# Reordering the first transfers, warming the array, widening the first stage and simplifying the first eight steps of a fused FNet and MLP kernel

## The chip, the cores and the metric

The kernel runs on one core of one Trainium2 chip. The metric is the device time of one execution in microseconds (us), as the median of several executions. Every run of a changed kernel is set against runs of the kernel before on the same chip in the same rounds. The engines are called PE (TensorE; PEld is its weight load), DVE (VectorE), ACT (ScalarE), POOL (GpSimd) and SP (the queue that issues most transfers).

## The reference

```python
# x (8, 3008, 256) float32; w_in (256, 2048) and w_out (2048, 256) are float64
X = np.fft.fft(np.fft.fft(x, axis=1), axis=2)
x = X.real.astype(np.float32).reshape(8 * 3008, 256)
h = x @ w_in
g = h * (1.0 / (1.0 + np.exp(-1.702 * h)))
out = (g @ w_out).astype(np.float32)
```

The random weights are scaled in float64 (NumPy promotes them) and arrive as float64. The kernel reads them as pairs of 32-bit words and rounds them to float32 on the chip.

## The kernel before

The sequence transform (3008 = 94 x 32) is split into a first stage, with 94 rows on the partitions and folded by symmetry, and a second stage of 32 points. The second transform, over the 256 columns, is folded into `w_in`: `fold_w` multiplies each rounded 512-column chunk of it by cosines and sines. Then 384 steps (8 batches x 3 blocks x 2 halves x 8 parts) compute 256 hidden units each and add their share to the output.

Weights come in eight chunks of 1 MB, four "in" and four "out". Each is rounded by five DVE operations with one ACT and two POOL operations around them:

```python
def bounds(key):
    hi = raw[key][:, :, 1].bitcast(F32)
    ...
    nc.scalar.activation(g[:], hi, ACTF.Square)
    nc.gpsimd.tensor_scalar(m[:], hi, scalar1=TOP, scalar2=-TOP, op0=ALU.min, op1=ALU.max)

def rounded(out, key):
    ...
    dve.scalar_tensor_tensor(m[:], g[:], LOW * LOW, m[:], op0=ALU.is_ge, op1=ALU.mult)
    dve.tensor_scalar(a[:], bits, scalar1=3, ...)                 # exponent
    dve.scalar_tensor_tensor(a[:], bits, 0xC0000000, a[:], ...)   # sign
    dve.scalar_tensor_tensor(a[:], lo, 29, a[:], ...)             # low bits
    dve.tensor_scalar(bits, lo, scalar1=28, scalar2=1, ...)       # round-up bit
    return lambda: nc.gpsimd.tensor_tensor(out.bitcast(U32), a[:], bits, op=ALU.add)
```

The first stage of batch 0 folds into `el` and `eu` (buffers of the pool `hp`, four in all) and multiplies with 96 columns of 94 rows:

```python
nc.tensor.matmul(ps[0:96, ...], lhsT=w1[:, l0, :], rhs=el[:, q, c0:c1], start=True, stop=False)
nc.tensor.matmul(ps[0:96, ...], lhsT=upper, rhs=eu[:, 3 - q, c0:c1], start=False, stop=True)
```

A step consists of `hidden(t)`, `product(t-2)`, `activate(t)` and, at the end of a half, `combine`. The order of these calls is the order of the instructions on each engine.

```python
def hidden(t):                       # pa, pb: 4 + 4 matmuls of 128x256
    ...
    nc.scalar.copy(v[:], pa[:])
    nc.vector.tensor_tensor(h[:, 0]..., v[:], pb[:], op=ALU.add)
    sums(t - 1)                      # Strassen's sums: two on POOL, two on DVE
    ...                              # two dif, one more h, all DVE
def product(t):                      # 7 products, 14 matmuls of 128x128, on wo and its differences wt
def combine(t):                      # 7 DVE operations at the end of each half of 8 steps

for t in range(n + LAG):
    hidden(t); product(t - LAG); activate(t); combine(t - LAG)   # guards cut
    for fn, args in extra.get(t, ()):                            # rounding, later batches
        fn(*args)
```

The start-up, before step 0:

```python
# w1, w1x on the ACT queue; then
load_first()                         # all of x[0], SP queue
load_in(0, nc.scalar); nc.scalar.dma_start(out=small[:], in_=tab2)
load_in(1, nc.scalar); load_out(0, nc.scalar)
...                                  # four times fold_first, mix_first
shuffle_first()                      # 12 transfers, SP
bounds(("in", 0)); bounds(("in", 1)); round_in(0); finish_in(0)
load_in(2, nc.sync)
fold_w(0)
...                                  # rounding of in 1 and out 0, second stage
```

Of the kernel before, what the change touches and what calls it, by code (L numbers as in the profile page):

```python
# [87 lines left out]
def kernel(ctx: ExitStack, tc, x, w_in, w_out, tab1, tab2, out):  # L88
# [22 lines left out]

    w1 = const.tile([NA, NW, 96], F32, tag="w1", name="w1")
    small = const.tile([128, 2 * 128 + 128 + 4 * H], F32, tag="small", name="small")
# [7 lines left out]
    af2 = const.tile([128, NF], F32, tag="af2", name="af2")  # L121
    ones = const.tile([1, 128], F32, tag="ones", name="ones")

    def bank(name):
# [49 lines left out]
    def mix1(b, c):  # L174
        full = xt[b]
        t, e = full[0:NA], e0.get(b)
        ps = bank("ps1")
        for i in range(2):
            jj, o = 2 * c + i, i * D
            if jj:  # L180
                nc.tensor.matmul(ps[0:96, o:o + D], lhsT=w1[:, jj, :], rhs=t[:, NB - jj, :], start=True, stop=True)  # L181
                continue
            for l0, l1, c0, c1 in ((0, 16, 0, H + 1), (17, 18, H + 1, D)):
                nc.tensor.matmul(ps[0:96, c0:c1], lhsT=w1[:, l0, :], rhs=e[:, 0, c0:c1], start=True, stop=False)
                nc.tensor.matmul(ps[0:96, c0:c1], lhsT=w1[:, l1, :], rhs=e[:, 1, c0:c1], start=False, stop=True)

        nc.scalar.copy(full[:, 2 * c:2 * c + 2, :].rearrange("p j d -> p (j d)"), ps[0:96, :])  # L187
# [3 lines left out]

    def load_first():
        t = xt[0] = xp.tile([96, NB, D], F32, tag="x", name="xt")
        src = x[0].rearrange("(p j) d -> p j d", j=NB)
        for c in range(4):
            for lo, hi in (((0, 4), (29, 32), (16, 17)), ((4, 8), (25, 29)), ((8, 12), (21, 25)), ((12, 16), (17, 21)))[c]:
                for p0, p1 in PIECES:
                    nc.sync.dma_start(out=t[p0:p1, lo:hi, :], in_=src[p0:p1, lo:hi, :])

    def fold_first(c):  # L200

        t = xt[0]
        el, eu = (hp.tile([NA, 4, D], F32, tag="h", name=n) for n in ("el", "eu"))
        e4[c] = el, eu
        first = 29 - 4 * c
        runs = [(el, 0, 4 * c, 4, False)]
        runs += [(eu, 0, first, 4, True)] if c else [(eu, 0, first, 3, True), (eu, 3, 16, 1, False)]
        for e, i, lo, n, flip in runs:
            fwd, rev = free(t[0:NA], lo * D + 1, [D, n], [1, H - 1]), free(t[0:NA], lo * D + D - 1, [D, n], [-1, H - 1])
            nc.gpsimd.tensor_copy(free(e[:], i * D, [D, n], [H, 2]), free(t[0:NA], lo * D, [D, n], [H, 2]))  # L210
            nc.vector.tensor_tensor(e[:, i:i + n, 1:H], fwd, rev, op=ALU.add)
            nc.vector.tensor_tensor(e[:, i:i + n, H + 1:D], *((rev, fwd) if flip else (fwd, rev)), op=ALU.subtract)

    def mix_first(c):
        ps = bank("ps1")
        el, eu = e4[c // 2]
        for i in range(2):
            jj, o = 2 * c + i, i * D
            q = jj % 4
            ends = ((0, 16, 0, H + 1), (17, 18, H + 1, D)) if jj == 0 else ((jj, NW + jj - 1, 0, D),)  # L220
            for l0, l1, c0, c1 in ends:
                upper = w1[:, l1, :] if l1 < NW else w1x[:, l1 - NW, :]
                nc.tensor.matmul(ps[0:96, o + c0:o + c1], lhsT=w1[:, l0, :], rhs=el[:, q, c0:c1], start=True, stop=False)
                nc.tensor.matmul(ps[0:96, o + c0:o + c1], lhsT=upper, rhs=eu[:, 3 - q, c0:c1], start=False, stop=True)
        nc.scalar.copy(xt[0][:, 2 * c:2 * c + 2, :].rearrange("p j d -> p (j d)"), ps[0:96, :])

    def shuffle_first():
        t4 = t4t[0] = tp.tile([128, NG, D], F32, tag="t4", name="t4")
        for a in range(NG):
            nc.sync.dma_start(out=t4[:, a, :], in_=xt[0][8 * a:8 * a + 8, 0:16, :])  # L230

# [51 lines left out]
    def bounds(key):  # L283


        hi = raw[key][:, :, 1].bitcast(F32)
        g = sp.tile([128, 1024], F32, tag="s", bufs=3, name="g")
        m = cv.tile([128, 1024], F32, tag="m", bufs=2, name="m")
        nc.scalar.activation(g[:], hi, ACTF.Square)
        nc.gpsimd.tensor_scalar(m[:], hi, scalar1=TOP, scalar2=-TOP, op0=ALU.min, op1=ALU.max)  # L290
        pre[key] = g, m

    def rounded(out, key):

        t, (g, m) = raw.pop(key), pre.pop(key)
        lo, bits = t[:, :, 0], m[:].bitcast(U32)
        a = cv.tile([128, 1024], U32, tag="a", name="a")
        dve = nc.vector
        dve.scalar_tensor_tensor(m[:], g[:], LOW * LOW, m[:], op0=ALU.is_ge, op1=ALU.mult)

        dve.tensor_scalar(a[:], bits, scalar1=3, scalar2=0x3FFFFFF8, op0=ALU.logical_shift_left, op1=ALU.bitwise_and)
        dve.scalar_tensor_tensor(a[:], bits, 0xC0000000, a[:], op0=ALU.bitwise_and, op1=ALU.bitwise_or)
        dve.scalar_tensor_tensor(a[:], lo, 29, a[:], op0=ALU.logical_shift_right, op1=ALU.bitwise_or)
        dve.tensor_scalar(bits, lo, scalar1=28, scalar2=1, op0=ALU.logical_shift_right, op1=ALU.bitwise_and)
        return lambda: nc.gpsimd.tensor_tensor(out.bitcast(U32), a[:], bits, op=ALU.add)

# [13 lines left out]

    def finish_out(n):
        ps = slice(2 * n, 2 * n + 2)
        last["out", n]()
        b11, b12, b21, b22 = (wo[:, ps, q, :] for q in range(4))
# [52 lines left out]
    def sums(t):  # L377

        if not 0 <= t < len(steps):
            return  # L380
# [9 lines left out]
    def product(t):  # L390
        b, blk, hh, p = steps[t]
        if p == 0:
            for n in range(4):
                pot[n] = pso.tile([128, 2, 2, H], F32, tag=f"o{n}", name=f"po{n}")
        h, s = ht.pop(t), st.pop(t)

# [13 lines left out]
    def combine(t):  # L410
# [5 lines left out]
        if hh == 0:  # L416
            for sg in range(2):
                ot[sg] = op.tile([128, 4, D], F32, tag="os", name="os")
        u2, u3, u4 = (op.tile([128, 2, H], F32, tag=f"u{n}", bufs=1, name=f"u{n}") for n in (1, 2, 3))
        c1 = pot["c"]  # L420
# [22 lines left out]
    assert NCK == 4  # L443
    w1x = tp.tile([128, NG, D], F32, tag="t4", name="w1x")[0:NA].rearrange("p a d -> p (a d)")[:, 0:NX * 96]
    w1x = w1x.rearrange("p (j n) -> p j n", j=NX)
    for p0, p1 in PIECES:
        nc.scalar.dma_start(out=w1[p0:p1], in_=tab1[p0:p1, 0:NW])
    for p0, p1 in PIECES:
        nc.scalar.dma_start(out=w1x[p0:p1], in_=tab1[p0:p1, NW:])
    load_first()  # L450
    load_in(0, nc.scalar)
    nc.scalar.dma_start(out=small[:], in_=tab2)
    load_in(1, nc.scalar)
    load_out(0, nc.scalar)
    nc.vector.memset(ones[:], 1.0)
    for c in range(4):
# [5 lines left out]
    mix_first(7)  # L462
    shuffle_first()
    bounds(("in", 0))
    bounds(("in", 1))
    round_in(0)
    finish_in(0)
    load_in(2, nc.sync)
    fold_w(0)
    bounds(("out", 0))  # L470
    round_in(1)
    finish_in(1)
    load_out(1, nc.sync)
    nyquist_weights(0)
    bounds(("in", 2))
    round_out(0)
    finish_out(0)
    load_in(3, nc.sync)
    rotate(0, 0, 4, nc.scalar.copy)
    for cs in range(2):  # L480
        stage2(0, 0, cs)
    nyquist(0, 0)

    extra = {}
# [5 lines left out]

    at(0, round_in, 2)
    at(0, load_out, 2, nc.sync)
    at(0, bounds, ("out", 1))
    at(1, fold_w, 1)
    at(1, nyquist_weights, 1)
    at(1, rotate, 0, 4, NG)
    at(1, finish_in, 2)
    at(1, round_out, 1)
    at(1, load_out, 3, nc.sync)
    at(1, bounds, ("in", 3))  # L500
    if B > 1:
        at(1, turn, 1, 17, 32)
        at(1, load_x, 1)
    at(2, finish_out, 1)
    at(2, round_in, 3)
    at(2, bounds, ("out", 2))
    at(3, fold_w, 2)
    at(3, nyquist_weights, 2)
    at(3, finish_in, 3)
    at(3, round_out, 2)  # L510
    at(3, bounds, ("out", 3))
    at(4, finish_out, 2)
    at(4, round_out, 3)
    at(5, fold_w, 3)
    at(5, nyquist_weights, 3)
    at(5, finish_out, 3)
    for b in range(B):
        t0 = b * NBLK * NF
        if b + 2 < B:
            at(t0 + 10, turn, b + 2, 17, 32)  # L520
        if b + 1 < B:
            for c in range(NCH):
                at(t0 + 7 + 2 * c, fold1, b + 1, c, nc.gpsimd)
                at(t0 + 8 + 2 * c, mix1, b + 1, c)
            at(t0 + 24, spill, b + 1)
            at(t0 + 29, fill, b + 1)
            if b + 2 < B:
                at(t0 + 33, load_x, b + 2)
            at(t0 + 38, rotate, b + 1)
        for blk in range(NBLK):  # L530
# [47 lines left out]
```

## Time and profile before

| | before |
|-|-|
| median of three runs | 2133.01 us (2132.48 to 2133.05) |
| span of the profiled run | 2130.3 us |
| end of stage 1 (end of its last matmul) | 41.1 us |
| first matmul of `fold_w` | 51.27 us |
| first matmul of step 6 | 146.32 us |

First the head of the page: busy us, share of the span and number of instructions for each engine. Below it are two of the rows that cut the span into 40 slices of 53 us, with the busy share (or, for PEclk, the granted clock) in tenths.

```profile
PE 2039.4 (96%) x14626; PEld 1912.7 (90%) x14626; DVE 1438.3 (68%) x2707; ACT 673.6 (32%) x952; POOL 774.7 (36%) x1058
...
PE   5669999999999999999999999999999999999998
...
PEclk9789999999999999999999999999999999999999
```

The average says that PE is the limit. The slices say that this holds from the fourth on; in the first three PE is busy five to six tenths. A change to the start-up is worth what it moves the beginning of the fourth slice.

The list of waits gives who waited for whom, then total us, times and the longest.

```profile
PE po L403 <- DVE u L426: 21.7, 16, 2.0
```

PE waits sixteen times, up to 2.0 us each, for the operations of `combine` on DVE; there are 48 halves, so every third of them has such a stall.

### The profile page before, as it was taken

How to read it: one execution, taken by the hardware profiler on the slowest of the kernel's cores; microseconds unless marked ns; L12 is line 12 of the kernel's file. 1: busy time of each engine (PE TensorE's matmuls, PEld its weight loads, DVE VectorE, ACT ScalarE, POOL GpSimd, SP SyncE). 2: the span in 40 equal slices, each digit the busy share in tenths (PEclk: the TensorE clock that was granted, in tenths of full speed). 3: DMA queues.
4: the chain of work that ended last, by engine and by line, in shares of the span. 5: the costliest groups of instructions: out<-in, count | busy, mean ns of one | idle time of the engine just before them, and what ended most of it. 6: DMA issues, size and time to landing. Idle time of an engine off the chain costs nothing.

```text
span 2130.3 us, 36302 instructions
## 1 busy us (share of the span) xinstructions
PE 2039.4 (96%) x14626; PEld 1912.7 (90%) x14626; DVE 1438.3 (68%) x2707; ACT 673.6 (32%) x952; POOL 774.7 (36%) x1058
## 2 busy tenths in 40 slices
PE   5669999999999999999999999999999999999998
PEld 3459999989999999999999899999999989999997
DVE  3676766766766667666666766676666667676666
ACT  1223323333233333333333333333333333323332
POOL 2465422353224522254223532244322542222222
PEclk9789999999999999999999999999999999999999
DMA  6341151123322033211431124111332112101200
GB/s 164 118 108 6 50 109 11 47 25 64 79 30 28 20 65 80 51 6 50 79 40 47 10 49 110 6 49 24 65 79 25 6 43 49 18 21 8 22 21 20
DMA packets 43263, 101.43 MB, mean 48 GB/s; under 512 B 4969, under 2 KB 27879, under 8 KB 41107
## 3 DMA queue, kind: packets, MB, share of 16 engines
q1 hardware_dynamic: 41631, 94.27, 24.0%
q10 hardware_dynamic: 1464, 4.83, 0.8%
q8 instruction: 115, 1.88, 0.4%
q14 instruction: 53, 0.43, 0.1%
HBM read 55.83 MB, written 45.76 MB: 48 GB/s over the span
## 4 chain that ended last, share of the span: by engine, by line
DVE 43%; PE 33%; issue 12%; ACT 9%; DMA 2%; SPq 1%; ACTq 0%; DVEq 0%; POOL 0%
PE po L403 19%; DVE dif L368 10%; DVE h L363 8%; DVE h L370 8%; DVE s L387 7%; DVE s L388 7%; ACT v L362 6%; PE pa L356 5%; PE pb L356 5%; DVE u L426 1%; PE ps L181 1%; DVE os L426 1%; ACT xt L187 1%; PE ps L253 1%; ACT pq L255 1%
## 5 line engine op out<-in xcount | busy, mean ns | idle before, releaser
L375 ACT ACTIVATE h<-h 128x1024 f32<-128x1024 f32 x384 | 405.9, 1057 | 1369.6 <-DVE h L370 1345.4
L385 POOL TENSOR_TENSOR s<-h 128x256 f32<-128x256 f32 x384 | 281.2, 732 | 1273.1 <-issue 930.7
L363 DVE TENSOR_TENSOR h<-v,pb 128x512 f32<-128x512 f32 x384 | 263.9, 687 | 614.8 <-ACT v L362 574.0
L403 PE MATMUL po<-wt,s 128*128 128x128 f32 x4608 | 644.5, 276 | 1.1 <-DVE s L387 1.1
L403 PEld LDWEIGHTS po<-wt,s 128*128 128x128 f32 x4608 | 580.5, 193 | 1.3 <-DVE s L387 1.3
L403 PE MATMUL po<-wo,h 128*128 128x128 f32 x3072 | 473.5, 277 | 23.2 <-DVE u L426 21.7
L403 PEld LDWEIGHTS po<-wo,h 128*128 128x128 f32 x3072 | 432.3, 192 | 56.6 <-DVE u L426 38.5
L356 PE MATMUL pa<-pq,wcs 128*128 128x256 f32 x1536 | 400.9, 384 | 0.0
L356 PE MATMUL pb<-pq,wcs 128*128 128x256 f32 x1536 | 397.9, 382 | 0.0
L368 DVE SCALAR_TENSOR_TENSOR dif<-nb,af,pb 128x256 f32<-128x256 f32 x768 | 332.0, 473 | 0.0
L356 PEld LDWEIGHTS pb<-pq,wcs 128*128 128x128 f32 x1536 | 294.8, 192 | 40.6
L356 PEld LDWEIGHTS pa<-pq,wcs 128*128 128x128 f32 x1536 | 268.5, 193 | 25.4 <-issue 1.5
L370 DVE TENSOR_TENSOR h<-v,dif 128x512 f32<-128x512 f32 x384 | 276.6, 720 | 13.2
L386 POOL TENSOR_TENSOR s<-h 128x256 f32<-128x256 f32 x384 | 283.4, 738 | 0.0
L387 DVE TENSOR_TENSOR s<-s,h 128x256 f32<-128x256 f32 x384 | 250.8, 653 | 2.0 <-POOL s L385 2.0
L403 PE MATMUL po<-wo,s 128*128 128x128 f32 x1536 | 234.8, 276 | 0.0
L403 PE MATMUL po<-wt,h 128*128 128x128 f32 x1536 | 234.6, 275 | 0.0
L362 ACT COPY v<-pa 128x512 f32<-128x512 f32 x384 | 219.4, 571 | 6.0 <-PE pa L356 6.0
L388 DVE TENSOR_TENSOR s<-h,s 128x256 f32<-128x256 f32 x384 | 206.6, 538 | 13.2
L403 PEld LDWEIGHTS po<-wo,s 128*128 128x128 f32 x1536 | 202.8, 193 | 0.0
L403 PEld LDWEIGHTS po<-wt,h 128*128 128x128 f32 x1536 | 202.7, 192 | 0.0
L169 POOL TENSOR_TENSOR xt<-xt 94x510 f32<-94x510 f32 (+1 forms) x56 | 73.8, 1318 | 4.4
(64 smaller groups left out, 749.4 us busy)
## 6 DMA issues: line engine op xcount, KB each, us to landing
out_dram<-os SPq DMA_DIRECT2D x176, 128.0 KB
Td<-xt SPq DMA_DIRECT2D x7, 1536.0 KB
t<-Td SPq DMA_DIRECT2D x7, 1536.0 KB
Xr<-in_x_dram SPq DMA_DIRECT2D x7, 1410.0 KB
xt<-in_x_dram SPq DMA_DIRECT2D x7, 1280.0 KB
xt<-Xr SPq DMA_DIRECT2D x7, 1200.0 KB
nb<-pq SPq DMA_DIRECT2D x23, 256.0 KB
raw<-in_moe_w_out_dram SPq DMA_DIRECT2D x3, 1024.0 KB
```

The costliest lines, as they stand in the source:

```text
L169: eng.tensor_tensor(low, low, free(t, up + D - 1, [-D, n], [-1, D - 1]), op=ALU.add)
L356: nc.tensor.matmul(ps[:, i * 256:(i + 1) * 256], lhsT=wcs[cs][:, f * 128:(f + 1) * 128], rhs=pq[:, cs, ks], start=True, stop=True)
L362: nc.scalar.copy(v[:], pa[:])
L363: nc.vector.tensor_tensor(h[:, 0].rearrange("p f k -> p (f k)"), v[:], pb[:], op=ALU.add)
L368: nc.vector.scalar_tensor_tensor(dif[:, c], nb[:, ks], af2[:, f:f + 1], pb[:, c], op0=ALU.mult, op1=ALU.subtract)
L370: nc.vector.tensor_tensor(free(h[:], 512 + NB - 1, [NB, 16], [-1, NB]), v[:].rearrange("p (a k) -> p a k", k=NB), dif[:].rearrange("p (a k ...
L375: nc.scalar.activation(ht[t][:], ht[t][:], ACTF.Gelu_apprx_sigmoid)
L385: nc.gpsimd.tensor_tensor(s1, a21, a22, op=ALU.add)
L386: nc.gpsimd.tensor_tensor(s3, a11, a21, op=ALU.subtract)
L387: nc.vector.tensor_tensor(s2, s1, a11, op=ALU.subtract)
L388: nc.vector.tensor_tensor(s4, a12, s2, op=ALU.subtract)
L403: nc.tensor.matmul(pot[n][:, i, q, :], lhsT=lhs[:, q * 128:(q + 1) * 128], rhs=rhs, start=(p == 0 and i == 0 and q == 0), stop=(p == NP - ...
```

## The change

The intent is to shorten the start-up:

- the first weight chunk is loaded ahead of `x` and rounded before stage 1; `small`, the second "in" chunk and the first "out" chunk are issued behind `x`, all on SP;
- eight matmuls on a tile of ones warm the array, and the first stage's weights are 128 columns wide;
- the two low-bit operations of the rounding leave DVE and become two ACT copies; the small fold copies go from POOL to ACT;
- the first eight steps use plain products (eight matmuls of 128x256) without Strassen's sums, and the differences `wt` move to steps 7 to 10;
- the folding of batch 1 in the background is shifted by three steps (its rotation by one step later; the rotation of the later batches moves two steps earlier).

```diff
+    load_in(0, nc.sync)
     for p0, p1 in PIECES:
-        nc.scalar.dma_start(out=w1[p0:p1], in_=tab1[p0:p1, 0:NW])
+        nc.scalar.dma_start(out=w1[p0:p1, 0:NW * 96], ...)
+    load_first(0)
     ...
+    for c in range(1, 4):
+        load_first(c)
+    nc.sync.dma_start(out=small[:], in_=tab2)
+    load_in(1, nc.sync)
+    load_out(0, nc.sync)
+    warm(8)
+    bounds(("in", 0))
+    round_in(0)
+    finish_in(0)
@@ mix_first
-                nc.tensor.matmul(ps[0:96, ...], lhsT=w1[:, l0, :], ...)
+                nc.tensor.matmul(ps[:, ...], lhsT=mat(w1, l0, 128), ...)
@@ bounds, rounded
+        nc.scalar.activation(r[:].bitcast(F32), lo, ACTF.Copy, scale=2.0 ** -29, bias=2.0 ** 23)
+        nc.scalar.activation(r[:], r[:].bitcast(F32), ACTF.Copy, bias=-2.0 ** 23)
-        dve.scalar_tensor_tensor(a[:], lo, 29, a[:], ...)
-        dve.tensor_scalar(bits, lo, scalar1=28, scalar2=1, ...)
@@ product
+        if t < NP:
+            ... 8 matmuls of 128x256: h[:, half, f] x wo[:, p, 2f:2f+2]
+            return
@@ combine
+        if t < NP:
+            ... two nc.scalar.copy
+            return
@@ background work of batch 1
+        late = 0 if b else 3
-                at(t0 + 7 + 2 * c, fold1, b + 1, c, nc.gpsimd)
+                at(t0 + 7 + 2 * c + late, fold1, b + 1, c, nc.gpsimd)
```

(Cut: the rest of the schedule of rounding, the zeroing of 32 columns behind the tables, two shuffles issued from ACT.)

## The prediction

> **What bounds the kernel now.** I read the page's head and 40 slices first: PE is busy 96% of 2130.3 us, and only the first three slices (some 160 us) are thin. Then I cut the span into windows; columns are window, length, then busy us with instruction counts for PE, PEld, DVE, ACT and POOL, then the granted clock, DMA share and GB/s.
>
> ```profile
> 20.00:40.00 20.00, 19.42 (x46) 12.55 (x45) 7.35 (x8) 5.25 (x8) 5.05 (x6) 1.00 0.60 170
> 40.00:60.00 20.00, 8.87 (x29) 4.52 (x27) 12.07 (x12) 4.99 (x7) 7.11 (x3) 1.00 0.35 74
> 60.00:80.00 20.00, 11.10 (x28) 7.80 (x29) 6.64 (x9) 5.60 (x8) 7.32 (x7) 0.57 0.51 163
> 80.00:100.00 20.00, 10.22 (x36) 7.50 (x35) 14.99 (x16) 5.48 (x9) 8.25 (x6) 0.66 0.18 52
> 100.00:120.00 20.00, 10.41 (x64) 7.94 (x62) 19.69 (x20) 3.23 (x4) 14.20 (x10) 0.82 0.90 245
> 120.00:140.00 20.00, 16.79 (x88) 13.67 (x88) 17.82 (x19) 4.72 (x8) 13.79 (x11) 0.84 0.39 108
> ...
> 160.00:180.00 20.00, 20.00 (x154) 19.12 (x153) 13.27 (x27) 7.88 (x13) 9.82 (x15) 1.00 0.02 2
> ...
> 500.00:1000.00 500.00, 493.54 (x3618) 468.24 (x3618) 341.43 (x657) 164.10 (x232) 185.66 (x262) 1.00 0.26 46
> ```
>
> From 160 us on, PE is busy 98% (1939 of 1970 us, summing all later windows), so that part ends when PE has done its work; nothing in the diff takes PE work out of it. The first 160 us are a start-up in which PE mostly waits. The whole question is how much earlier the saturated part begins. As marker I take the instant at which PE starts the two 128x256 groups `pa` of step 6 (last one that needs a freshly folded weight chunk): 146.32 us in the timeline below. From there PE runs without a gap at 4.85 us a step.
>
> The timeline of the start (start us, duration, engine, line, what, count, idle before and releaser):
>
> ```profile
> 26.34 1.06 PE L223 MATMUL ps<-el,w 94*96 94x256 f32 x2
> 27.19 1.06 PE L224 MATMUL ps<-eu,w1x 94*96 94x256 f32 x2
> ...
> 51.27 5.44 PE L333 MATMUL psw<-wst,small 128*128 128x512 f32 x8 [10.20 <-POOL wst L305]
> ...
> 58.80 1.12 SPq L273 DMA_DIRECT2D raw<-in_moe_w_in_dram  x1
> ...
> 67.00 1.12 ACT L289 ACTIVATE g<-raw 128x1024 f32<-128x1024 f32 x1 [8.36 <-DMA raw<-in_moe_w_in_dram]
> ...
> 68.02 0.15 ACT L245 COPY t<-psr 128x4 f32<-128x4 f32 x1
> ...
> 75.08 0.58 ACT L362 COPY v<-pa 128x512 f32<-128x512 f32 x1 [1.42 <-PE pa L356]
> ...
> 81.55 1.63 DVE L302 SCALAR_TENSOR_TENSOR a<-m,a 128x1024 uint32<-128x1024 uint32 x1
> 83.21 1.23 DVE L303 SCALAR_TENSOR_TENSOR a<-raw,a 128x1024 uint32<-128x1024 uint32 x1
> 84.36 0.69 DVE L304 TENSOR_SCALAR m<-raw 128x1024 uint32<-128x1024 uint32 x1
> ...
> 85.19 2.34 POOL L305 TENSOR_TENSOR wst<-a,m 128x1024 uint32<-128x1024 uint32 x1 [3.09 <-DVE m L304]
> 85.55 2.26 DVE L387 TENSOR_TENSOR s<-s,h 128x256 f32<-128x256 f32 x1
> ...
> 146.32 2.08 PE L356 MATMUL pa<-pq,wcs 128*128 128x256 f32 x4
> ```
>
> The reader is to see four things. (1) The first stage's 94x256 matmuls start 0.85 us apart, while the same form in the saturated part (L181) takes 0.43; stage 1 therefore lasts to 41.1 us. (2) Step 0 begins late: ScalarE sits behind a 1 MB weight chunk issued at 58.80 (it lands at 67.0), and the tiny copy at 68.02, which the second stage needs, stands behind it in order. (3) Step 0's `v` copy comes at 75.08. (4) Steps 0 to 6 take 71.2 us (75.08 to 146.32) because VectorE rounds weight chunks between the steps: five operations, 1.2+0.7..1.2+1.2..1.6+1.2..1.6+0.7 = about 5.9 us a chunk, plus its `s` operation of 0.42 stretched to 2.26 under GpSimd's 2.34 us addition. The wait list says the same: PE's largest wait is for the folded weights.
>
> ```profile
> PE psa L339 <- ACT wcs L334: 27.8, 4, 11.0
> ```
>
> **What the Trainium skill says.** "TensorE: Matmul & The Clock Gate", Part 1 (the HAM clock gate): the array runs at half rate until it has been busy for about 3.4 us and falls back after an idle window. The trace agrees at L333: its eight halves are 0.85 apart for about 3.5 us, then 0.43. It does not agree for stage 1, 27 us of unbroken 94x96 work at half rate (and the clock column calls that window 1.00). I read this as 96 of 128 columns being too little activity to release the gate; no page says so. The same page, Architectural detail: ScalarE is a strict FIFO; the 68.02 copy shows it. "SBUF — State Buffer", on the shared port pair: a GpSimd operation holds the pair for its whole length and a VectorE one with two SBUF inputs blocks; 85.55 shows it (2.26 for 0.42). "DMA: Bandwidth & Descriptors", Issuing engines are not separate DMA queues: SP and ACT feed the same 16 engines, so reordering helps only by what goes first; the first 20 us agree, with the DMA share at 0.93.
>
> **The change part by part.**
>
> *First transfers.* The first weight chunk goes ahead of x, and the second weight chunk, `small` and the first output chunk go behind it. Bytes up to the last piece of x: 1.05 + 0.67 + 0.53 + 3.08 = 5.3 MB; at the 226 to 300 GB/s of the first 30 us that is 20 to 23 us plus start and landing, so about 25.5 us against 31.15 before. Chunk 0 of x is later, though (7.8 before; 11 to 13.5 now, behind 1 MB), and VectorE first does three roundings (9.3 to 13.8), so stage 1 starts at about 15 to 17 rather than 8.6 to 13.
>
> *Warming and width.* Eight warm-up matmuls of 128x512: four halves cold, twelve warm, about 1.5 to 10 us, off the path. A gap of about 5 us follows, so I expect chunk 0 of stage 1 to begin cold and turn warm within 4 us if 128 columns are enough: 16.9 + 5.1, then three chunks of 8 x 0.43 = 3.4 us: end at about 32.5 (41.1 before, gain 8.6). If the gate stays shut, 16.9 + 32 x 0.85 = 44: a loss of 3.
>
> *From stage 1 to step 0.* Before: 34 us. Now the first chunk is already rounded (the fold waited 10.2 us for it), and what is left is a ScalarE queue: two shuffle issues 2.8, two `wcs` copies 1.1, `bounds` of chunk 1 (now a Square and two copies of 128x1024, 3 x 1.1 = 3.3), second-stage copies and waits with a cold PE 5.7, `bounds` of the first output chunk 3.3, and the 0.6 until the last stage-1 copy: 17. So `v` at about 50 (75.08 before): 25 earlier.
>
> *Steps 0 to 6.* Rounding leaves VectorE (three operations, 3.1 to 4 us) but ScalarE gets 2.2 us more a chunk, and in its order `bounds` stands between one step's Gelu and the next step's `v`. That makes a ring, per step: bounds 3.3, v 0.57, VectorE's h, two dif and h 2.3 (`sums` is gone for t<8), Gelu 1.06: 7.2 us, above PE's 1.73 + 3.46 = 5.2. From `v` of step 0: 4.0, five rings 36.2, the two weight turns inside (copies 1.05, bias matmuls 1.05, waits 0.35) 4.9, the last turn up to `pa` 2.2, the wait for chunk 2 (issued after ten shuffle issues of 1.4 from 33, so landing near 55) 1.3, port collisions 1.5: 50. So step 6 starts near 100 us against 146.3: 46 earlier.
>
> *After step 6.* Plain products are 8 matmuls of 128x256, 8 x 0.433 = 3.46, against 14 x 0.223 = 3.12: +0.34 for each of products 4 to 7, +1.4. The group of step 6 was cold before (3.6 against 1.7): -1.9. The first combine on VectorE, where PE waited 1.80 at 215 us, becomes two ScalarE copies: -1.8. Moving the `wt` differences to steps 7 to 10 puts some 12 us on GpSimd, whose own step work is 1.5 of 4.9; I expect it to catch up before PE starves: 0. Fold and rotation of later batches are merely shifted: 0.
>
> Sum: -46.3 + 1.4 - 1.9 - 1.8 = -48.6, hence 2084.4.
>
> **The rivals.** (a) *The gate stays shut in stage 1.* For it: 94 of 128 rows are still idle in part, PE has gaps at each x chunk, and 27 us of 94x96 never opened it. Against: someone padded to 128 for this and nothing else, and full-size matmuls opened it in 3.5 us. I give it one in four; it costs 11.5: about 2096. (b) *ScalarE becomes the bound of the start more than I count.* It takes VectorE's two roundings and GpSimd's small copies, and any slow read of the unsigned words at a stride of two, or a table load per kind of function, would lengthen the 7.2 us ring; 0.5 us a chunk is 3 us in all: 2087 to 2090. Against: the Square of the same shape and stride takes 1.13 and brought no table load. (c) *Transfers take the place.* Chunk 2 still waits behind the shuffles on SP; if the 2.5 MB queued behind x delay the shuffles, step 0 moves by up to 5: 2090. Against: DMA share is 0.35 in 40 to 60. (d) *Hidden anyway.* If later steps were limited by something else, nothing would come out; PE at 98% with no slack speaks against it: a microsecond in the start is a microsecond at the end. (e) *Better than counted:* if the warm-up holds through the gap and x lands at 24, stage 1 ends near 29 and PE's share is shorter everywhere: 2077.
>
> **Range and chances.** Three in four for a warm stage 1 around 2084 with a spread of 7; one in four around 2096. Together about 2087. The 2% line is 2133.0 x 0.98 = 2090.3, so it lies inside the range: 2073 to 2102. Faster by over 2%: 0.6; within: 0.395; slower: 0.005, since I see no part that lengthens the saturated 1980 us.
>
> **What would show it.** Right: stage-1 matmuls 0.43 apart from the second chunk on and their end near 32; step 0's `v` near 50; ScalarE's order Gelu, three `bounds`, `v` with PE waiting on it at about 7.2 us a step; step 6 near 100; then 5.2 us a step up to step 9 and 4.85 after; PE busy within 160 us of the end unchanged. Wrong: stage-1 matmuls still 0.85 apart; steps 0 to 6 much shorter or longer than 50 us; PE gaps of several us around steps 9 to 12 on GpSimd's `s`; or a different total in the later batches.

## The result, and the profile after

The changed kernel takes 2108.41 us (median, 2107.39 to 2109.01) against 2132.86 (2132.48 to 2133.05) for the kernel before in the same rounds. The ratio is 0.9885, with a 95% interval of 0.9868 to 0.9902. The change gains 24.5 us: same within 2%, and outside the predicted range on the slow side.

The head and the slices of the page of the changed kernel:

```profile
PE 2047.6 (97%) x14546; PEld 1918.2 (91%) x14546; DVE 1402.0 (67%) x2669; ACT 693.2 (33%) x978; POOL 748.6 (36%) x1035
...
PE   7799999999999999999999999999999999999998
...
PEclk6899999999999999999999999999999999999999
```

PE is now thin in two slices instead of three, and the first slice's clock digit has fallen from 9 to 6. The windows of the start (us; columns as in the prediction: PE, PEld, DVE, ACT, POOL, clock, DMA share, GB/s):

```profile
20.00:40.00 20.00, 18.50 (x46) 14.36 (x47) 7.70 (x15) 2.74 (x8) 1.10 (x1) 0.50 0.59 185
...
120.00:140.00 20.00, 20.00 (x90) 17.45 (x89) 7.95 (x14) 6.06 (x8) 11.04 (x15) 0.91 0.00 1
```

PE is full from 120 us on instead of 160. From 20 to 40 us it is busy 18.5 of 20 us, yet completes only 46 matmuls: it is busy, but slowly. The timeline of the start shows it, from the warm-up on (start us, duration, engine, line, what, count, idle before and releaser):

```profile
1.46 10.09 PE L239 MATMUL warm<-wcs 128*128 128x512 f32 x16 [1.46 <-DVE wcs L474]
...
12.42 1.12 ACT L299 ACTIVATE g<-raw 128x1024 f32<-128x1024 f32 x1 [3.69 <-DMA raw<-in_moe_w_in_dram]
...
17.40 2.82 DVE L213 TENSOR_TENSOR el<-xt 94x508 f32<-94x508 f32 x1
...
17.57 0.77 PE L225 MATMUL ps<-el,w 94*128 94x129 f32 x2 [6.03 <-issue]
...
21.50 0.77 PE L226 MATMUL ps<-eu,w 94*128 94x129 f32 x2 [3.15 <-DVE eu L212]
...
26.32 1.06 PE L225 MATMUL ps<-el,w 94*128 94x256 f32 x2
27.18 1.06 PE L226 MATMUL ps<-eu,w1x 94*128 94x256 f32 x2
...
27.48 0.68 DVE L212 TENSOR_TENSOR eu<-xt 94x508 f32<-94x508 f32 x1 [4.73 <-issue]
...
48.97 5.01 PE L347 MATMUL psw<-wst,small 128*128 128x512 f32 x8
...
68.05 0.57 ACT L376 COPY v<-pa 128x512 f32<-128x512 f32 x1
...
118.79 1.13 PE L370 MATMUL pa<-pq,wcs 128*128 128x256 f32 x4
```

The warm-up ends at 11.55, and PE then idles 6.03 us and, after one matmul, 3.15 us; in finer windows the clock column falls from 1.00 to 0.50 between 14.0 and 14.5 us, within the first of these gaps. The first weight chunk reaches ACT at 12.42. The fold at L213 takes 2.82 us, where the same form takes 0.68 (L212), because POOL's addition of the rounding runs over it. The fold of `eu` waits 4.73 us for a buffer, behind matmuls that are slow (the profile names no releaser for it, but ACT's copy into the same buffer, at 27.47, waited for L225). Stage 1's matmuls are 0.85 apart, exactly as before. `fold_w` starts right behind them, at 48.97: stage 1 ends some 8 us later than before, yet the fold begins 2.3 us earlier (51.27 before), since its weights are already rounded. And its 128-row matmuls turn warm within these 5.01 us (their weight loads start 0.85 apart up to 51.53 and 0.43 apart from 52.10), right behind 27.5 us of 94-row matmuls that did not. From there the lead grows: `v` of step 0 comes at 68.05 (75.08 before), step 6 at 118.79 (146.32 before).

The largest wait of PE, for the folded weights, has fallen from 27.8 us to 11.7. The stalls behind `combine` are as they were:

```profile
PE psa L353 <- ACT wcs L348: 11.7, 4, 8.8
PE po L427 <- DVE u L454: 22.9, 15, 2.0
```

The milestones, in us from the start of the span, with the predicted values beside them:

| | before | predicted | after |
|-|-|-|-|
| stage 1 ends | 41.1 | 32.5 | 48.97 |
| `v` of step 0 | 75.08 | 50 | 68.05 |
| step 6 starts | 146.32 | 100 | 118.79 |
| from step 6 to the end of the span | 1984.0 | 1981.7 | 1987.4 |
| span | 2130.3 | about 2082 | 2106.2 |

Stage 1 to `v` took 19.1 us (17.5 predicted), and `v` to step 6 took 50.7 (50 predicted). What is wrong sits in two rows: the end of stage 1 is 16.5 us late, and the tail is 5.7 us longer than predicted.

### The profile page after: what moved, and what is told of

It is laid out like the page before. It is cut to its first block, busy times and chain, and to the rows that moved or that the text cites. A ratio compares the mean times of both kernels' runs of the same rounds, so it can differ in the third digit from the quotient of the medians.

```text
span 2106.2 us, 36069 instructions
## 1 busy us (share of the span) xinstructions
PE 2047.6 (97%) x14546; PEld 1918.2 (91%) x14546; DVE 1402.0 (67%) x2669; ACT 693.2 (33%) x978; POOL 748.6 (36%) x1035
## 4 chain that ended last, share of the span: by engine, by line
PE 42%; DVE 37%; issue 10%; ACT 8%; POOL 0%; DMA 0%; ACTq 0%; DVEq 0%; SPq 0%; POOLq 0%
PE po L427 24%; DVE dif L382 8%; DVE h L384 7%; DVE h L377 7%; PE pa L370 7%; PE pb L370 6%; DVE s L401 6%; DVE s L402 6%; ACT v L376 5%; PE ps L262 1%; DVE u L454 1%; PE ps L184 1%; DVE os L454 1%; ACT xt L190 1%; PE po L415 1%
## 5 line engine op out<-in xcount | busy, mean ns | idle before, releaser
L399 POOL TENSOR_TENSOR s<-h 128x256 f32<-128x256 f32 x376 | 273.4, 727 | 1245.6 <-issue 919.3
L427 PE MATMUL po<-wt,s 128*128 128x128 f32 x4512 | 632.8, 277 | 1.1 <-DVE s L401 1.1
L427 PEld LDWEIGHTS po<-wt,s 128*128 128x128 f32 x4512 | 570.1, 193 | 1.3 <-DVE s L401 1.3
L427 PE MATMUL po<-wo,h 128*128 128x128 f32 x3008 | 463.6, 277 | 24.0 <-DVE u L454 22.9
L427 PEld LDWEIGHTS po<-wo,h 128*128 128x128 f32 x3008 | 423.5, 192 | 54.9 <-DVE u L454 36.9
L400 POOL TENSOR_TENSOR s<-h 128x256 f32<-128x256 f32 x376 | 273.6, 728 | 0.0
L401 DVE TENSOR_TENSOR s<-s,h 128x256 f32<-128x256 f32 x376 | 241.0, 641 | 3.3 <-POOL s L399 3.3
L427 PE MATMUL po<-wo,s 128*128 128x128 f32 x1504 | 230.4, 276 | 0.0
L427 PE MATMUL po<-wt,h 128*128 128x128 f32 x1504 | 229.9, 276 | 0.0
L402 DVE TENSOR_TENSOR s<-h,s 128x256 f32<-128x256 f32 x376 | 200.2, 532 | 12.9
```

The source lines that it names most:

```text
L399: nc.gpsimd.tensor_tensor(s1, a21, a22, op=ALU.add)
L400: nc.gpsimd.tensor_tensor(s3, a11, a21, op=ALU.subtract)
L401: nc.vector.tensor_tensor(s2, s1, a11, op=ALU.subtract)
L402: nc.vector.tensor_tensor(s4, a12, s2, op=ALU.subtract)
L427: nc.tensor.matmul(pot[n][:, i, q, :], lhsT=lhs[:, q * 128:(q + 1) * 128], rhs=rhs, start=(p == 0 and i == 0 and q == 0), stop=(p == NP - ...
```

## The experiments

The questions, and the theories that compete for each:

1. *Why is stage 1 cold?* Cold means that its matmuls of 256 columns start 0.85 us apart, warm that they start 0.43 apart; what switches between the two is called the gate here, as in the prediction. Either too few **rows** of the array are at work (94 of 128) to open the gate, or the idle time between warm-up and stage 1 (6.03 us, then 3.15) and the small gaps are what keeps it shut (**gap**), or something in the **width** of 128 columns does.
2. *What sets the 50 us to step 6?* The **ring** through ACT (three `bounds` operations between Gelu and the next `v`), or the collision of DVE and POOL, or the transfers.
3. *Where did the tail's 5.7 us go?* The **shift** of batch 1's folds, the differences on POOL, or the plain products.

The expectations use letters for theories as working labels; the text under each result names them by content. Twelve kernels ran, on three chips, and all gave correct results.

| run | median (range), us | before, us | ratio (95%) | gain, us |
|-|-|-|-|-|
| the change | 2108.41 (2107.39–2109.01) | 2132.86 | 0.9885 (0.9868–0.9902) | 24.5 |
| cols96 | 2108.31 (2107.33–2109.81) | 2134.09 | 0.9880 (0.9865–0.9895) | 25.8 |
| rows128 | 2100.35 (2099.71–2101.99) | 2134.09 | 0.9843 (0.9828–0.9858) | 33.7 |
| bridge20 | 2096.14 (2095.65–2098.49) | 2134.09 | 0.9826 (0.9809–0.9842) | 38.0 |
| cols96_bridge | 2098.07 (2096.93–2098.68) | 2133.92 | 0.9833 (0.9819–0.9848) | 35.9 |
| vfirst | 2103.20 (2102.16–2105.10) | 2134.09 | 0.9856 (0.9842–0.9871) | 30.9 |
| noplain | 2117.60 (2116.67–2118.51) | 2133.92 | 0.9927 (0.9910–0.9943) | 16.3 |
| dveround | 2113.25 (2112.34–2115.57) | 2133.92 | 0.9907 (0.9892–0.9921) | 20.7 |
| late0 | 2107.97 (2105.84–2110.29) | 2133.92 | 0.9880 (0.9866–0.9895) | 26.0 |
| oldorder | 2118.21 (2113.50–2119.88) | 2134.09 | 0.9921 (0.9904–0.9937) | 15.9 |
| combo_b | 2100.70 (2099.47–2101.59) | 2134.09 | 0.9845 (0.9830–0.9859) | 33.4 |
| combo_c | 2094.06 (2093.80–2095.23) | 2133.65 | 0.9815 (0.9799–0.9832) | 39.6 |
| combo_a | 2092.88 (2092.83–2100.95) | 2134.09 | 0.9818 (0.9800–0.9836) | 41.2 |

The gain is the difference of the two medians in the row. All are same within 2%, except combo_c, whose interval crosses the line. The differences between variants are the gains' differences.

### cols96: the width alone undone

```diff
-                upper = mat(w1, l1, 128) if l1 < NW else mat(w1x, l1 - NW, 128)
-                nc.tensor.matmul(ps[:, ...], lhsT=mat(w1, l0, 128), ...)
+                upper = mat(w1, l1) if l1 < NW else mat(w1x, l1 - NW)
+                nc.tensor.matmul(ps[0:96, ...], lhsT=mat(w1, l0), ...)
```

> The changed kernel with the first stage 96 columns wide again. Theories A and B both say that the width does nothing alone: matmuls 0.85 us apart, first stage ends near 49, time 2107 to 2110. If the width did help somewhere (the reading of the prediction), this is slower than the changed kernel.

It gains 25.8 us, the change 24.5; its matmuls are 0.85 apart up to the end of stage 1 at 48.13, and step 6 starts at 118.66 (118.79). Thirty-two more columns are worth nothing when the array is cold.

### rows128: all 128 rows, the upper ones zero

```diff
-    w1 = const.tile([NA, NW * 96 + 32], F32, tag="w1", name="w1")
+    w1 = const.tile([128, NW * 96 + 32], F32, tag="w1", name="w1")
+    def rows(c):
+        pair = tuple(hp.tile([128, 4, D], F32, tag="h", name=n) for n in ("el", "eu"))
+        for e in pair:
+            nc.gpsimd.memset(e[64:128], 0.0)
+        return pair
```

> The first stage of the changed kernel with all 128 rows of the array in use: its tables and folded x are padded with zero rows 94 to 127, nothing else. Theory A (the clock gate opens only when nearly the whole array is in use, and 94 rows are too few): matmuls start 0.85 us apart at first and 0.43 apart after 4 to 7 us of them, the first stage ends near 37 instead of 49 us, the time is near 2097. Theory B (the gate counts the unbroken time of work, and the short stops of the first stage or the idle 6 us ahead of it keep it shut): still 0.85 apart to the end near 49 to 50 us, time 2107 to 2110.

The timeline of PE in stage 1:

```profile
18.49 0.77 PE L232 MATMUL ps<-eu,w 128*128 128x129 f32 x2 [3.15 <-DVE eu L218]
...
20.76 0.91 PE L232 MATMUL ps<-eu,w1x 128*128 128x256 f32 x2
21.51 0.59 PE L231 MATMUL ps<-el,w 128*128 128x256 f32 x2
21.94 0.59 PE L232 MATMUL ps<-eu,w1x 128*128 128x256 f32 x2
...
37.09 0.67 PE L232 MATMUL ps<-eu,w1x 128*128 128x256 f32 x2 [2.56 <-DVE eu L219]
...
39.31 1.06 PE L232 MATMUL ps<-eu,w1x 128*128 128x256 f32 x2
40.16 1.06 PE L231 MATMUL ps<-el,w 128*128 128x256 f32 x2
```

With gaps of 4.57 and 3.15 us before it (6.03 and 3.15 in the changed kernel), and with the clock column at 0.50 from 15 us, stage 1 with 128 rows turns warm about 3 us after its start: starts are 0.85 apart up to 20.76 and 0.43 from 21.51. In the changed kernel 27.5 us of 94 rows never did. So the shape decides whether the gate opens, and it is the rows. PE then outruns the folds and waits 1.66, 1.66 and 2.56 us; after the last of these the rate is halved again from 38.46, and stage 1 ends at 41.87. From the first `eu` matmul this is 23.4 us instead of 27.5.

One thing is mixed in: a DVE zeroing of the tables' upper rows delayed the tables' transfer (issued at 3.60 instead of 0.74), the weight chunk landed by 6.36 instead of 12.42, ACT took it up at 9.42, behind a table load, and stage 1 began 3 us earlier. The gain of 9.2 over the change contains that. What holding the tables back is worth by itself no run tests.

### bridge20: twenty warm-up matmuls instead of eight

```diff
-    warm(8)
+    warm(20)
```

> Twenty warm-up matmuls instead of eight, so that they run up to about 21.3 us, where the first stage starts in earnest; nothing else. Theory A (94 rows are too little activity): the first matmuls of the first stage start 0.43 us apart, but the gate shuts again within [...]some 4 to 7 us, and the rest are 0.85 apart; first stage ends near 45, time 2104 to 2107. Theory B (warmth was lost in the idle time ahead of the stage): 0.43 apart throughout, first stage ends near 36, time near 2096.

```profile
1.46 19.06 PE L239 MATMUL warm<-wcs 128*128 128x512 f32 x40 [1.46 <-DVE wcs L474]
...
22.17 0.60 PE L225 MATMUL ps<-el,w 94*128 94x256 f32 x2
22.60 0.59 PE L226 MATMUL ps<-eu,w1x 94*128 94x256 f32 x2
...
37.38 0.59 PE L226 MATMUL ps<-eu,w1x 94*128 94x256 f32 x2
37.81 3.60 PE L347 MATMUL psw<-wst,small 128*128 128x512 f32 x8
```

With only 0.68 us of idle time left between warm-up and stage 1, the same 94-row matmuls run 0.43 apart for all of stage 1, through gaps of 0.66 us, and it ends at 37.81 instead of 48.97. The gain over the change is 13.5 us (38.0 against 24.5) for the 11.2 us that stage 1 ends earlier. So 94 rows cannot open the gate but keep it open, and the gap of the changed kernel was the other half of the cause. This is the one-line version that beats both kernels.

### cols96_bridge: 96 columns with the bridge

The edit is that of cols96 and that of bridge20 together.

> First stage 96 columns wide again, with twenty warm-up matmuls. The run with twenty showed that 94 rows by 128 columns keep an open gate open for 16 us though they cannot open it. Theory A2 (what keeps it open is the share of the array in use, and 94 by 96 falls below it): first-stage matmuls fall back to 0.85 us apart within 4 to 7 us, time 2102 to 2107. Theory E (any steady matmuls keep it open, so the width is worth nothing here either): 0.43 apart throughout, time 2095 to 2098 as with 128 columns.

```profile
38.24 0.59 PE L225 MATMUL ps<-el,w 94*96 94x256 f32 x2
38.67 0.59 PE L226 MATMUL ps<-eu,w1x 94*96 94x256 f32 x2
```

These are its last stage-1 matmuls: 96 columns also stay at 0.43 to the end, at 39.1 us. The gain is 2.1 us below that of bridge20, which ran on another chip; its stage 1 ends 1.3 us later at the same rate. At 94 rows the width of 128 does nothing, neither cold nor warm.

### vfirst: `v` ahead of the rounding's ACT operations

```diff
+    early = {1: [("in", 2)], 2: [("out", 1)], 3: [("in", 3)], 4: [("out", 2)], 5: [("out", 3)]}
@@ hidden, behind nc.scalar.copy(v[:], pa[:])
+        for key in early.pop(t, ()):
+            bounds(key)
@@ schedule
-    at(0, bounds, ("in", 2))        # and the four other bounds
```

> In steps 1 to 5 ScalarE makes the copy v of the step before the three operations on the next raw weight chunk, not after them; nothing else. Theory C (ScalarE's order Gelu, three operations, v, with VectorE waiting, is a ring of 7 us that sets the pace of the steps 0 to 6): the ring falls to PE's 5.2 us, step 6 starts near 110 instead of 118.8, time near 2099 to 2101. Rival D (PE, VectorE's rounding or GpSimd's additions set that pace): step 6 within 2 us of 118.8, time 2106 to 2109.

First the changed kernel's ring, from its timeline of steps 0 and 1 (two of the three `bounds` operations cut):

```profile
72.41 1.06 ACT L389 ACTIVATE h<-h 128x1024 f32<-128x1024 f32 x1 [2.50 <-DVE h L384]
73.44 1.14 ACT L299 ACTIVATE g<-raw 128x1024 f32<-128x1024 f32 x1
...
76.58 0.57 ACT L376 COPY v<-pa 128x512 f32<-128x512 f32 x1
77.18 0.69 DVE L377 TENSOR_TENSOR h<-v,pb 128x512 f32<-128x512 f32 x1 [4.80 <-ACT v L376]
...
79.41 1.06 ACT L389 ACTIVATE h<-h 128x1024 f32<-128x1024 f32 x1 [2.26 <-DVE h L384]
```

Gelu to Gelu takes 7.0 us, the ring of 7.2 that the prediction worked out, with DVE idle 4.80 us in it. Now vfirst, the same part of a later step:

```profile
91.24 0.56 ACT L377 COPY v<-pa 128x512 f32<-128x512 f32 x1
91.70 1.18 ACT L299 ACTIVATE g<-raw 128x1024 f32<-128x1024 f32 x1
...
94.62 2.37 POOL L317 TENSOR_TENSOR wo<-a,r 128x1024 uint32<-128x1024 uint32 x1
94.84 2.71 DVE L387 TENSOR_TENSOR h<-v,dif 128x512 f32<-128x512 f32 x1
```

`v` now comes first, but the last `h` of the step takes 2.71 us instead of 0.69, under POOL's addition of the rounding. Step 6 starts at 116.34, where I expected 110 (118.79 in the change), and step 6 itself takes 5.29 us instead of 6.97. The gain over the change is 6.4 us (30.9 against 24.5), of which 4.1 are there at step 8 (126.81 against 130.94); I cannot place the other 2.3. The ring is real, but taking it away shows the collision and DVE's own rounding right behind it.

### noplain: Strassen's products in the first eight steps too

```diff
-        if not NP <= t < len(steps):
+        if not 0 <= t < len(steps):
-        if t < NP:                   # in product and in combine
+        if t < 0:
```

(The differences go back behind `finish_out` of their chunk.)

> The changed kernel with the seven-product scheme from step 0 on: sums in every step, the differences of wo made as soon as a chunk is rounded. If plain products pay because they take sums off VectorE and GpSimd while these round (the prediction's view): steps 2 to 7 become longer by 1 to 2.5 us each, less 0.35 us per product for PE, so slower than the changed kernel by 5 to 12 us: 2113 to 2120. If ScalarE alone paces these steps, sums are hidden: 2105 to 2109.

It loses 8.2 us of gain (16.3 against 24.5); step 6 starts at 131.49, 12.7 later than in the change, of which the later steps give 4.5 back. Its timeline shows why the sums cost so much there:

```profile
101.09 2.54 POOL L317 TENSOR_TENSOR wo<-a,r 128x1024 uint32<-128x1024 uint32 x1
101.45 2.47 DVE L402 TENSOR_TENSOR s<-h,s 128x256 f32<-128x256 f32 x1
```

An `s` of 0.42 us lasts 2.47 under the rounding's addition, as in the kernel before. Plain products add 0.34 us of PE work a step, measured as predicted (5.18 us a step against 4.85 once PE is full), and take this operation out of the way while weights are rounded. The run also brings the differences back into the start: POOL works on them from 103.71 to 108.09, where a rounding operation of DVE takes 1.74 us instead of 1.22. How the 12.7 us divide between sums and differences it does not show.

### dveround: the low bits on DVE again

```diff
-        nc.scalar.activation(r[:].bitcast(F32), lo, ACTF.Copy, scale=2.0 ** -29, bias=2.0 ** 23)
-        nc.scalar.activation(r[:], r[:].bitcast(F32), ACTF.Copy, bias=-2.0 ** 23)
+        dve.scalar_tensor_tensor(a[:], lo, 29, a[:], ...)
+        dve.tensor_scalar(bits, lo, scalar1=28, scalar2=1, ...)
```

(The buffers of `m` and `r` go back with it.)

> The changed kernel with the low bits rounded by two more VectorE operations again instead of two ScalarE ones. Theory C (the ring through ScalarE, 7 us a step, paces steps 1 to 6): ScalarE's part falls to 5 us but VectorE's rises from 5.6 to 7.6, so about even or a little slower: 2106 to 2112. If the move to ScalarE was the main gain of the start: slower by 8 or more, 2116 and up.

It gains 20.7 us, so sharing the rounding is worth about 4 (24.5 less 20.7). Step 6 starts at 125.08, 6.3 later than in the change. Two operations of 1.2 and 0.7 us for seven chunks would be some 13 us of DVE (an estimate from the rows that the prediction shows), so under half of that comes out. The two copies that ACT gets in exchange cost 2.2 us a chunk in its ring, which may be why; this run alone does not show it.

### late0: the folds of batch 1 not shifted

```diff
-        late = 0 if b else 3
+        late = 0
```

> The folds of the second batch of x start at step 7 as before, not at step 10; nothing else. If the shift made GpSimd's fold collide with the combine near 230 us, where PE now waits 1.8 us it did not wait before: 1 to 2 us faster, 2106 to 2107.5. If the differences of wo and the folds now collide in steps 7 to 10: 2 to 6 us slower. Even: the shift is worth nothing.

It gains 26.0 against 24.5, within the spread. Step lengths (from one step's first `pa` to the next one's) say what happens:

| step | before | after | late0 |
|-|-|-|-|
| 8 | 7.05 | 6.07 | 7.38 |
| 10 | 6.61 | 6.08 | 7.83 |
| 18 | 7.84 | 6.69 | 7.87 |
| 26 | 6.05 | 7.84 | 6.04 |

The shift moves a stall rather than removing it. Without it steps 8, 10 and 18 are long; with it step 26 is. In the changed kernel the stall of step 26 reads so:

```profile
234.36 0.41 DVE L454 TENSOR_TENSOR u<-u,po 128x256 f32<-128x256 f32 x1
...
234.83 0.71 PE L427 MATMUL po<-wo,h 128*128 128x128 f32 x4 [1.77 <-DVE u L454]
```

PE waits 1.77 us for a `combine` operation on DVE, of the same kind as the 1.80 at 215 us that the prediction meant to save. That one, in the kernel before, was in step 18:

```profile
216.89 0.71 PE L403 MATMUL po<-wo,h 128*128 128x128 f32 x4 [1.80 <-DVE u L426]
```

### oldorder: the transfers in the old order, rounding behind stage 1

```diff
-    load_in(0, nc.sync)              # first; likewise the bounds and rounding of in 0
-    nc.sync.dma_start(out=small[:], in_=tab2)
-    load_in(1, nc.sync)
-    load_out(0, nc.sync)
+    load_in(0, nc.scalar)            # behind x, on the ACT queue
+    nc.scalar.dma_start(out=small[:], in_=tab2)
+    load_in(1, nc.scalar)
+    load_out(0, nc.scalar)
@@ behind the shuffles
+    bounds(("in", 0)); round_in(0); finish_in(0)
```

> The changed kernel with the transfers in the old order (tables and x first, weight chunks behind) and the first chunk rounded after the first stage, as before. Prediction's view: stage 1 starts 6 to 8 us earlier and, being cold, ends near 41 to 43 instead of 49, but the fold of the weights then waits some 7 us for the rounding; so within 3 us of the changed kernel: 2105 to 2111. If the order of need was worth more than that: 2112 or more.

I expected 2105 to 2111 and measured 2118.21, with a spread of 6 us among its runs. The miss has its own cause:

```profile
20.33 0.38 ACTq L287 DMA_DIRECT2D raw<-in_moe_w_out_dram  x1
...
22.04 0.21 ACT L211 COPY el<-xt 94x8 f32<-94x8 f32 x1
22.30 0.80 PE L225 MATMUL ps<-el,w 94*128 94x129 f32 x2 [12.23 <-ACT el L211]
```

The small fold copies are on ACT now, and ACT issues its last transfer only at 20.33, so the fold's last piece waits behind the issues and PE idles 12.23 us. Stage 1 then runs cold to about 49.8, and the rounding comes after it. So this run does not isolate the order of transfers: it measures the order together with freeing ACT of issuing, worth about 8.6 us together (24.5 less 15.9).

### combo_a, combo_b, combo_c: towards a better version

combo_a is bridge20 with `v` ahead of the rounding from step 0 on, the first "out" chunk rounded in step 0, and the third "in" chunk issued ahead of the last eight shuffles:

```diff
-    warm(8)
+    warm(20)
+    early = {0: [("out", 0)], 1: [("in", 2)], 2: [("out", 1)], 3: [("in", 3)], 4: [("out", 2)], 5: [("out", 3)]}
     shuffle_first(nc.scalar, 2, 3)
+    load_in(2, nc.sync)
     shuffle_first(nc.sync, *range(4, NG))
```

> Twenty warm-up matmuls, every v ahead of the ScalarE operations on raw chunks from step 0 on, and the third raw chunk issued ahead of the last eight shuffle transfers. If the gains add (12 us from the open gate, 5 from the order of ScalarE, 3.3 for the chunk that stood ahead of the first v): 2086 to 2091. If they share one path: 2091 to 2096.

It is the best version: 2092.88 us, 41.2 below the kernel before in its rounds; step 6 starts at 105.36. One of its four runs took 2100.95, at a granted clock of 0.988 instead of 0.994; I did not find out which part of the start lost those 8 us. The chunk between the shuffles was not free: PE's first matmul on the shuffled rows started at 51.03, in bridge20 at 47.62.

combo_b is combo_a with an earlier stage 1: the rounding of chunk 0 comes behind the first folds, `wst(0)` gets another buffer so that the folds keep all four, and 14 warm-ups suffice. It also folds the second weight chunk in step 0 instead of step 1 (cut here):

```diff
-    round_in(0)
-    finish_in(0)
     for c in range(4):
         fold_first(c)
+        if c == 1:
+            round_in(0)
+            finish_in(0)
```

> As combo_a, and: the second weight chunk is folded in step 0 instead of step 1, so that step 2 no longer waits for a second Gelu; the first chunk is rounded after the folds of x's first two chunks, and its tile no longer takes one of the four buffers that the folds rotate through; fourteen warm-up matmuls. If step 2 now starts 7 us earlier and stage 1 ends near 32: 2070 to 2080. If the rounding collides with the folds: 2080 to 2090.

```profile
23.56 0.59 PE L225 MATMUL ps<-el,w 94*128 94x256 f32 x2
24.00 0.59 PE L226 MATMUL ps<-eu,w1x 94*128 94x256 f32 x2
...
24.46 2.64 POOL L317 TENSOR_TENSOR wst<-a,r 128x1024 uint32<-128x1024 uint32 x1 [10.66 <-DVE a L316]
24.82 2.82 DVE L213 TENSOR_TENSOR el<-xt 94x508 f32<-94x508 f32 x1
...
27.79 1.19 PE L225 MATMUL ps<-el,w 94*128 94x256 f32 x2 [3.20 <-DVE el L213]
...
40.21 1.06 PE L225 MATMUL ps<-el,w 94*128 94x256 f32 x2
41.06 1.06 PE L226 MATMUL ps<-eu,w1x 94*128 94x256 f32 x2
```

Up to 24 us its stage 1 ran 0.43 apart. Then POOL's addition held one fold for 2.82 us, PE waited 3.20 us, and the 94-row matmuls behind that gap were 0.85 apart for 14 us, until 41.92. This is the cleanest demonstration of the mechanism: the same matmuls in the same run are warm before one gap and cold after it, and cannot get out of it by themselves. The clock column falls between 27 and 28 us, at the end of the gap. The version loses 7.8 us to combo_a: 3.5 of them are there at the end of stage 1 (41.92 against 38.42), 7.3 at step 6 (112.66 against 105.36). Whether the moved fold has a share in the rest no run tells.

combo_c is combo_a with the third "in" chunk issued right behind the first "out" chunk, at about 23 us, when the queue is free:

```diff
     load_out(0, nc.sync)
+    load_in(2, nc.sync)
```

> As combo_a (twenty warm-up matmuls, every v ahead of the ScalarE operations on raw chunks), but the third raw chunk is issued right behind the first output chunk at about 23 us, so that it lands before 40 us, while the transfer engines stood idle from 33 to 40 us in both earlier runs, and not between the shuffles, whose landing it delayed from 47.6 to 51.0 us. If that delay is all that held combo_a back: shuffles land near 48, step 0 starts near 54, step 6 near 103, time 2088 to 2091. If the shuffles are no faster: as combo_a, 2092 to 2094.

PE's first matmul on the shuffled rows started at 48.19, as expected and 2.8 us earlier than in combo_a, and step 0 began 1.5 us earlier (55.04 against 56.53). But its first three groups of matmuls in step 0 took 1.9 to 2.1 us each where combo_a's took 1.0 to 1.1, and step 6 began at 105.96, later than combo_a's 105.36. The result is even: 39.6 against 41.2. Why one of the two finds the array warm at step 0 and the other does not, no run here tests.

## Why the prediction was wrong

The predicted gain was 46 us (2133.0 less 2087), or 48.6 by the main sum; the measured one is 24.5. Going through the prediction's steps:

**What bounds the kernel**, right. A microsecond saved in the start was a microsecond at the end, nearly: the changed kernel leads by 27.5 us at step 6 and by 24.1 at the end of the span.

**First transfers**, about right in order, late in size: the weight chunk reached ScalarE only at 12.42, VectorE's roundings ran from 13.66 to 16.87 instead of 9.3 to 13.8, and the first complete pair of stage-1 matmuls started at 21.5 rather than 16.9. About 2.1 us of that are the fold that POOL's addition held to 2.82 us; the first fold of `eu` came right behind it, at 20.14. (The sum of bytes also gives 18 to 23 us at the rates named, not 20 to 23.)

**Warming and width: this is the step that failed.** I wrote that stage 1 would "turn warm within 4 us if 128 columns are enough". The warm-up itself ran longer than I counted, some seven halves cold instead of four, to 11.55 instead of 10, and the gap behind it was 6.03 and 3.15 us instead of 5. The stage ended at 48.97 instead of 32.5: 4.6 us from the late start and 11.9 from the rate (27.5 us from the first `eu` matmul instead of the 15.6 that I summed). The runs show what stands in its place. Width is nothing at 94 rows (cols96, cols96_bridge). Ninety-four rows do not open a shut gate (27.5 us in the changed kernel, 14 us in combo_b). 128 rows do, in about 3 us (rows128). And 94 rows keep an open gate open as long as the gaps are short (bridge20). I had named the rival "the gate stays shut" and given it one in four at 2096, with the 94 rows as its first argument; the mechanism I gave in the main line, columns, was the wrong dimension of the same matmul. The cost was also larger than the rival's: stage 1 ended at 49, not 44, since the rival took over the start at 16.9. The trace of before could have warned me: 94 rows and 96 columns were both short of 128 there, so a cold stage 1 spoke for the one as much as for the other.

**From stage 1 to step 0**, right: 19.1 us for 17.5.

**Steps 0 to 6**, right in the sum: 50.7 us for 50, with the ring of 7.0 us seen in the trace for the 7.2 worked out. The sum fits in part by luck: no wait for chunk 2 came (1.3 us counted), while collisions with POOL stretched the last `h` of four steps by some 3 us in all (1.5 counted). vfirst shows that the ring was not alone: the collision of DVE and POOL stood close behind it, so that taking the ring apart brought step 6 forward by 2.4 us and not by the 8.8 that I expected.

**After step 6: the second step that failed**, by 5.7 us. Predicted was 1.4 - 1.9 - 1.8 = -2.3; measured +3.4 (1987.4 less 1984.0).
- "+0.34 for each of products 4 to 7" held: 5.18 us a step.
- "The group of step 6 was cold before: -1.9" did not come. Step 6 took 6.94 us before and 6.97 after. In the changed kernel product 4 waits in that step for POOL's addition of the third "out" chunk (119.05 to 121.42).
- "The first combine: -1.8" was put down to the wrong combine. The stall at 215 us belongs to step 18, which is behind the second half of eight steps, where the products are still Strassen's. Step 18 did get shorter (7.84 to 6.69), and step 26 longer (6.05 to 7.84).
- "Fold and rotation of later batches are merely shifted: 0" was right for the total (late0 is even), but it is what moves the stall to step 26.
- The marker was read too simply: the prediction has PE run "without a gap at 4.85 us a step" from 146.32 on, but steps 6, 8 and 10 of the kernel before took 6.94, 7.05 and 6.61 us.
- The rest of the loss, from a lead of 25.1 at step 48 to 24.1 at the end, is within the 1.6 us by which runs of the changed kernel differ.

**The other rivals.** ACT as the bound (b) is visible in the ring; the one table load in these steps, 1.28 us at 68.63, was hidden, since Gelu waited another 2.50 us for DVE behind it. Transfers taking the place (c) are visible in the first weight chunk, some 3 us late, but not in chunk 2, which the rival named: ACT took it up at 73.44 without a wait, just as it landed. Better than counted (e) is what bridge20 comes nearest to: its stage 1 ends at 37.81 and not near 29, since its warm-up is there but `x` and the rounding hold the start to 21.4.

Left open: whether the gate goes by rows or by a share of the array's activity (only 94x96, 94x128 and 128x128 ran); what the eight warm-ups alone are worth (no run without them); why combo_a lost 8 us in one run; and why eight to nine us pass from the last stage-1 copy to PE's first matmul on the shuffled rows.

## What to carry to other kernels

A cold array is a state, and a tuned start-up must be read for where it is lost: look at the spacing of equal matmuls, since the busy share does not show it and the clock column read 1.00 over cold matmuls here up to its first fall, and bridge any gap before a partly filled matmul with filler of full size, which costs nothing while PE waits anyway. When work is moved from a busy engine to an idle one, check what stands behind it in order there: moving two operations of the rounding to ACT brought 4 us of the 13 that they took, and moving small copies to ACT made them wait for the issue of transfers when that queue was in use. Before a stall is counted as saved, find which step owns it and which background work sets its place, since such a stall moves on more often than it goes.

## What the Trainium skill lacked or had wrong

- "TensorE: Matmul & The Clock Gate", Part 1, tells the warm-up as a matter of busy time alone (about 3.4 us). Here the filling counts: 94 of 128 rows, with 96 or 128 columns, did not open the gate in 27 us, 128 rows did in about 3 us, and 94 rows held it open for 16 us. The 128 rows did so with the upper 34 of them zero.
- The same part puts the fall back to half rate behind an idle window of about 3.4 us. Here 0.66 us gaps did not cause it, and one of 3.20 us, shorter than that window, did for 94 rows (the page's closing table says about 3 us, which fits); with 128 rows two waits of 1.66 us were survived, and half rate came 1.4 us after one of 2.56. The page calls the window free-running, and the runs agree that the instant varies: the same eight warm-ups, started at 1.46 each time, have their weight loads 0.43 apart from 4.69 us on in rows128, from 5.03 in vfirst and from 7.52 in the changed kernel. Whether that is also why gaps of different lengths shut the gate, no run here shows.
- The page's HAM trace caveats say that recorded events can be unreliable; no page says where the clock column of a profile misleads. Here it reads 1.00 from the start of the span to its first fall, whatever the spacing: in the kernel before up to 60 us, over 27 us of matmuls 0.85 apart, and in the changed kernel over the cold first 6 us of its warm-up. In the windows looked at after the first fall it agrees with the spacing (0.50 from 20 to 40 us in the changed kernel).
